# The inverse table's copy and clearing on VectorE, and the first weight loads dealt out anew

## The chip, the cores and the metric

One core of a Trainium2 chip runs the kernel. The metric is the device time of one execution in microseconds (us). The kernel before takes 508.08 us, the median of three runs (507.65, 508.08 and 508.6).

## The reference

The reference is a forward pass and its gradients. Sequence length is S = 2048, width D = 512, hidden width F = 1376, all in bf16.

```python
xn = layernorm(q)                                     # [2048, 512]
kv = v * sum_t k[s - t] * shift_k[:, t]               # 4 taps
y  = causal_conv(kv, ssm_k) + kv * ssm_D              # by FFT of length 4096, per channel
h  = sigmoid(xn @ w_gate) * (xn @ w_up)               # [2048, 1376]
out = q + (xn * y) * silu(h @ w_down)
# outputs: out, and with grad_out the gradients of
# q, k, v, shift_k, ssm_k, ssm_D, w_gate, w_up, w_down
```

## The kernel before

**Recording and ordering.** The kernel body does not emit instructions directly. Each call such as `nc.vector.tensor_copy` goes to a recorder (`Rec.add`), which notes what it reads and writes. At the end `Rec.order` simulates the five engines with a table of estimated durations, picks an order for every engine, chooses the PSUM banks and, for evacuations of PSUM (`evac`), the engine (ScalarE or VectorE). `Rec.emit` then writes the instructions in that order. So an edit to one engine or one DMA queue can change the order of instructions on all engines, as long as the planned times differ. In the profile nearly all instructions carry the line of the emitter, L568, and matmuls carry L566.

**Stages.** First come constants (sine and cosine tables for the FFT, made by `gen_fft_consts`), layer normalisation of q (`f_ln`), the gate and up projections (`f_gen`, in eight groups of 256 tokens) and the forward convolution (`strK` for the filter, `strV` for the signal, both with an FFT written as matmuls). All these streams are interleaved. Then `stepB` does the backward pass of the gated part, group by group: `z_gen` (down projection and silu gradient), `d_gen` (gradient of h), `x_gen` (gradient of xn). At last the weight gradients (`dW`) run beside the backward convolution (`frontC`, `backC`).

**The inverse table.** The backward convolution multiplies by `RT2`, a table of 128 partitions by 2 by 128 elements, built in `RT2_gen` during `stepB`, when the third group of `d_gen` has been recorded. A copy of a single element per partition (from `dzA`, into `RT2`) only serves as a dependency: it keeps the clearing from being placed before that part of `dzA` is written. Then the table is cleared, and four ScalarE copies of 32 partitions each fill in blocks of the first table `RT`. Before the change, the single-element copy and the clearing run on GpSimd. The table itself is used only much later, in `inv3w`.

**The first loads.** `ld_w(eng, f0, f1)` loads columns f0 to f1 of w_gate and w_up on the DMA queue of `eng`, as two DMAs. Before the change the columns 0 to 512 and 512 to 1024 are loaded on ScalarE's queue (four DMAs of 512 KB each), the rest (1024 to 1376, two DMAs of 352 KB) on SyncE's queue, behind the first 256 KB of q (`f_x(0)`) and the filter (`ld_KT(0)`, 512 KB). Two tiny loads, the column ssm_D (`Dcol_b`, 1 KB) and the shift weights (`skT`, 4 KB), run on GpSimd's queue, ssm_D first. The shift weights are used in `strV` by the VectorE multiply that builds `dg4` (128x512 elements); ssm_D is added to the filter by GpSimd in `strK`. GpSimd also computes the power −1/2 in `f_ln`, one instruction of 128x1 per 128 tokens, between VectorE's statistics and VectorE's normalisation. The transposed load of k (`ld_kT(0)`) is made to wait, through a single-element GpSimd copy, for the last part of w_up.

Of the kernel before, what the change touches and what calls it, by code (L numbers as in the profile page):

```python
# [17 lines left out]
P = 128  # L18
# [641 lines left out]
def kernel_impl(ctx, tc, A_q, A_k, A_v, A_shift_k, A_ssm_k, A_ssm_D, B_x, B_w_gate, B_w_up, B_w_down,  # L660
                grad_out, out_0, out_1, out_2, out_3, out_4, out_5, out_6, out_7, out_8, out_9):
    nc = tc.nc
# [34 lines left out]
    RT2 = Ring(ar, [2, 128]).ap  # L697
# [4 lines left out]
    skT = Ring(ar, [NG, 4]).ap  # L702
# [29 lines left out]
    def f_x(q):  # L732
        T[q]["xq"] = wd[:, 0:2, :] if q == 1 else xq_r.next()
        dma2(nc.sync, T[q]["xq"], qC[:, :, 2 * q:2 * q + 2, :])
# [172 lines left out]
    def ld_KT(cg):  # L907
        stA["KT", cg] = KT_r.next()
        nc.sync.dma_start(stA["KT", cg], A_ssm_k[cg * GW:(cg + 1) * GW, :])
# [19 lines left out]
    def ld_w(eng, f0, f1):  # L929
        for w, src in ((wg, B_w_gate), (wu, B_w_up)):  # L930
            eng.dma_start(w[:, :, f0:f1], src[:, f0:f1].rearrange("(db p) f -> p db f", p=P))
# [6 lines left out]
    nc.vector.memset(neghalf, -0.5)  # L938
    f_x(0)
    ld_w(nc.scalar, 0, 512)  # L940
    ld_w(nc.scalar, 512, 1024)
    nc.gpsimd.dma_start(Dcol_b, A_ssm_D.rearrange("(cg p) -> p cg", p=P))
    nc.gpsimd.dma_start(skT, A_shift_k.rearrange("(cg p) t -> p cg t", p=P))
    ld_KT(0)
    ld_w(nc.sync, 1024, F)
    f_x(1)
    nc.gpsimd.tensor_copy(kT[:, 16:17], wu[:, 3, F - 1:F])
# [186 lines left out]
    BQ = [6, 7, 3, 0, 4, 1, 5, 2]  # L1134
# [15 lines left out]
    dzA = dz_r.ap  # L1150
# [102 lines left out]
            nc.scalar.copy(skb[:, :, db * 128:(db + 1) * 128], pb[:].rearrange("p (d t) -> p t d", t=4))  # L1253

    def RT2_gen():
        nc.gpsimd.tensor_copy(RT2[:, 0, 0:1], dzA[:, 2 * BQ[1], 0:1])
        nc.gpsimd.memset(RT2, 0.0)
        for r in range(4):
            h = slice(32 * r, 32 * r + 32)
            nc.scalar.copy(RT2[h, :, 64 * (r % 2):64 * (r % 2) + 64], RT[h, 0:2, :])  # L1260

    def stepB():
        yield from z_gen(BQ[0])
        yield from z_gen(BQ[1])
        for n, q in enumerate(BQ):
            yield from d_gen(q)
            if n in (2, 3, 7):
                flags.add("d%d" % n)
                yield 1
            if n + 2 < 8:  # L1270
                b_ld(BQ[n + 2])
                b_ldg(BQ[n + 2])
            if n == 2:
                skb_gen()
                RT2_gen()
            if 1 <= n < 7:
                yield from z_gen(BQ[n + 1])
            if n == 6:
                flags.add("z15")
                yield 1  # L1280
            yield from x_gen(q)
            if n + 3 < 8:
                f_ld(BQ[n + 3])
            if n == 5:
                flags.add("x5")
                yield 1
# [244 lines left out]
@with_exitstack  # L1531
def kernel(
    ctx: ExitStack,
    tc: tile.TileContext,
    A_q: bass.AP,
    A_k: bass.AP,
    A_v: bass.AP,
    A_shift_k: bass.AP,
    A_ssm_k: bass.AP,
    A_ssm_D: bass.AP,  # L1540
    B_x: bass.AP,
    B_w_gate: bass.AP,
    B_w_up: bass.AP,
    B_w_down: bass.AP,
    grad_out: bass.AP,
    out_0: bass.AP,
    out_1: bass.AP,
    out_2: bass.AP,
    out_3: bass.AP,
    out_4: bass.AP,  # L1550
    out_5: bass.AP,
    out_6: bass.AP,
    out_7: bass.AP,
    out_8: bass.AP,
    out_9: bass.AP,
):
    kernel_impl(tc, A_q, A_k, A_v, A_shift_k, A_ssm_k, A_ssm_D, B_x, B_w_gate, B_w_up, B_w_down,
                grad_out, out_0, out_1, out_2, out_3, out_4, out_5, out_6, out_7, out_8, out_9)
# [30 lines left out]
```

## Time and profile before

| | |
|---|---|
| median of 3 runs | 508.08 us |
| lowest, highest | 507.65, 508.6 us |
| the profiled execution | 513.07 us, span 511.3 us, granted clock 0.983 |
| instructions | 13658 |
| TensorE busy | 462.3 us (90% of the span) |
| VectorE busy | 393.8 us (77%) |
| ScalarE busy | 274.9 us (54%) |
| GpSimd busy | 27.9 us (5%) |
| DMA moved | 112.74 MB, mean 221 GB/s |

In the profile PE is TensorE's matmuls, PEld its weight loads (which overlap the matmuls), DVE is VectorE, ACT ScalarE, POOL GpSimd and SP SyncE; ACTq, POOLq and SPq are the DMA queues of these engines, or their sequencers. The start of a line is its time in us from the span's start and its length; what stands in brackets at the end is the engine's idle time before it, and what ended that. A granted clock below 1 is TensorE running slower than it can. A profiled execution is some 5 us longer than the runs without a profile.

### The profile page before, as it was taken

How to read it: one execution, taken by the hardware profiler on the slowest of the kernel's cores; microseconds unless marked ns; L12 is line 12 of the kernel's file. 1: busy time of each engine (PE TensorE's matmuls, PEld its weight loads, DVE VectorE, ACT ScalarE, POOL GpSimd, SP SyncE). 2: the span in 40 equal slices, each digit the busy share in tenths (PEclk: the TensorE clock that was granted, in tenths of full speed). 3: DMA queues.
4: the chain of work that ended last, by engine and by line, in shares of the span. 5: the costliest groups of instructions: out<-in, count | busy, mean ns of one | idle time of the engine just before them, and what ended most of it. 6: DMA issues, size and time to landing. Idle time of an engine off the chain costs nothing.

```text
span 511.3 us, 13658 instructions
## 1 busy us (share of the span) xinstructions
PE 462.3 (90%) x5862; PEld 303.4 (59%) x5895; DVE 393.8 (77%) x658; ACT 274.9 (54%) x344; POOL 27.9 (5%) x50
## 2 busy tenths in 40 slices
PE   2999989999999967999999999999888869978997
PEld 2776857586758544565566556445454545656665
DVE  6788989758775695887998998649765789995770
ACT  5759787667665664144464257147544765164121
POOL 4101100000000031000000000100000000000000
PEclk9899999999999997999999999999998999999999
DMA  9999999946599988788969788995989898985666
GB/s 250 232 245 302 275 212 248 266 166 197 195 241 242 240 186 160 241 231 249 288 197 272 199 193 197 238 258 202 196 201 244 194 203 228 229 202 134 161 209 198
DMA packets 173813, 112.74 MB, mean 221 GB/s; under 512 B 101621, under 2 KB 157881, under 8 KB 173752
## 3 DMA queue, kind: packets, MB, share of 16 engines
q1 hardware_dynamic: 171288, 109.37, 86.0%
q10 hardware_dynamic: 2112, 2.10, 1.5%
q8 instruction: 46, 0.75, 0.6%
q0 software_dynamic: 352, 0.40, 0.3%
q14 instruction: 15, 0.12, 0.1%
HBM read 39.23 MB, written 47.62 MB: 170 GB/s over the span
## 4 chain that ended last, share of the span: by engine, by line
PE 72%; DVE 10%; issue 6%; DMA 5%; ACT 5%; POOL 2%; ACTq 0%; DVEq 0%; POOLq 0%
PE psum L566 72%; DVE slab L568 10%; ACT slab L568 5%; DMA slab<-slab 2%; DMA slab<-in_B_w_up_dram 2%; POOL slab L568 2%; DMA slab<-in_B_w_gate_dram 1%; PE psum L568 0%; ACTq L568 0%; DVEq L568 0%; POOLq L568 0%
## 5 line engine op out<-in xcount | busy, mean ns | idle before, releaser
L566 PE MATMUL psum<-slab 128*128 128x256 bf16 (+10 forms) x5853 | 460.9, 265 | 45.5 <-ACT slab L568 25.4
L566 PEld LDWEIGHTS <-slab 128*128 128x128 bf16 (+5 forms) x5886 | 302.7, 102 | 203.1 <-issue 67.7
L568 ACT CAST slab<-psum 128x1024 bf16<-128x1024 f32 (+6 forms) x263 | 216.6, 874 | 173.8 <-PE psum L566 157.7
L568 DVE TENSOR_TENSOR slab<-slab 128x1024 bf16<-128x1024 bf16 (+4 forms) x344 | 243.1, 759 | 36.6 <-ACT slab L568 18.3
L568 DVE CAST slab<-psum 128x1024 bf16<-128x1024 f32 (+1 forms) x31 | 36.7, 1187 | 31.7 <-PE psum L566 18.5
L568 ACT ACTIVATE slab<-psum 128x1024 bf16<-128x1024 f32 (+2 forms) x44 | 37.3, 854 | 32.2 <-PE psum L566 29.1
L568 DVE TENSOR_TENSOR slab<-psum,slab 128x1024 bf16<-128x1024 f32 (+2 forms) x28 | 28.2, 1006 | 13.4 <-PE psum L566 11.0
L568 DVE STREAM_TRANSPOSE slab<-slab 128x512 f32<-128x512 f32 x48 | 30.8, 684 | 3.6 <-ACT slab L568 3.5
L568 ACT ACTIVATE slab<-slab 128x512 bf16<-128x512 bf16 (+3 forms) x25 | 21.7, 888 | 16.4 <-DVE slab L568 16.3
L568 DVE SCALAR_TENSOR_TENSOR slab<-slab 128x512 bf16<-128x512 bf16 (+1 forms) x48 | 24.7, 530 | 3.9 <-ACT slab L568 3.4
L568 DVE TENSOR_SCALAR slab<-slab 128x1 f32<-128x1 f32 (+8 forms) x58 | 13.7, 270 | 1.4 <-POOL slab L568 0.9
L568 POOL TENSOR_TENSOR slab<-slab 128x1 f32<-128x1 f32 (+1 forms) x20 | 9.9, 509 | 77.8 <-DVE slab L568 66.2
L568 DVE BATCH_NORM_STATS2 slab<-slab 128x6 f32<-128x512 bf16 x16 | 10.3, 681 | 4.2 <-DMA slab<-in_A_q_dram 4.2
L568 POOL MEMSET slab<- 128x128 bf16 (+4 forms) x8 | 3.4, 429 | 174.5 <-PE psum L566 133.1
L568 POOL DMA_DIRECT2D slab<-slab x8 | 4.3, 535 | 153.3 <-DVE slab L568 153.3
L568 DVE SCALAR_TENSOR_TENSOR slab<-psum,slab 128x512 bf16<-128x512 f32 x10 | 6.7, 686 | 4.3 <-PE psum L566 4.3
L568 POOL COPY slab<-slab 128x1 bf16<-128x1 bf16 x2 | 6.9, 3426 | 48.4 <-DVE slab L568 42.9
L568 DVE COPY slab<-slab 128x1216 bf16<-128x1216 bf16 (+2 forms) x16 | 7.1, 460 | 1.1 <-ACT slab L568 1.1
L568 ACT ACT_TABLE_LOAD x2 | 2.6, 1283 | 5.7 <-DMA slab<-in_B_w_gate_dram 5.7
L568 ACT COPY slab<-slab 32x128 bf16<-32x128 bf16 x4 | 1.2, 295 | 5.4 <-POOL slab L568 5.3
L568 DVE MEMSET slab<- 32x192 uint32 (+2 forms) x7 | 1.1, 165 | 1.9 <-PEq L1573 0.8
L568 DVE BATCH_NORM_AGGREGATE slab<-slab 128x2 f32<-128x6 f32 x16 | 2.4, 170 | 0.0
(15 smaller groups left out, 11.5 us busy)
## 6 DMA issues: line engine op xcount, KB each, us to landing
KK_d<-slab SPq DMA_DIRECT2D x16, 512.0 KB, 4.0
slab<-KK_d SPq DMA_DIRECT2D x16, 512.0 KB, 5.2
out_dram<-slab SPq DMA_DIRECT2D x58, 128.0 KB, 3.2
hS_d<-slab SPq DMA_DIRECT2D x8, 704.0 KB, 5.8
dgS_d<-slab SPq DMA_DIRECT2D x8, 704.0 KB, 4.8
duS_d<-slab SPq DMA_DIRECT2D x8, 704.0 KB, 5.5
sF_d<-slab SPq DMA_DIRECT2D x6, 704.0 KB, 5.6
slab<-sF_d SPq DMA_DIRECT2D x6, 704.0 KB, 5.7
```

Of the source, the lines that this page charges most:

```text
L566: getattr(self.nc.tensor, m)(*[place(v) for v in aa], **{x: place(v) for x, v in kk.items()})
L568: getattr(getattr(self.nc, eng), meth)(*[place(v) for v in a], **{x: place(v) for x, v in k.items()})
```

## The change

In `RT2_gen` the single-element copy and the clearing move from GpSimd to VectorE. At the start, the weight columns 512 to 1024 are loaded on SyncE's queue, behind the filter and ahead of the columns from 1024 on, so that ScalarE's queue keeps two DMAs of 512 KB. On GpSimd's queue the shift weights are loaded ahead of ssm_D. Nothing else in the source changes. The order that the recorder finds does change: on TensorE from the 137th to about the 926th matmul, on the other engines in the same part and around the inverse table. Of the PSUM evacuations, two of 128x1024 elements are now given to ScalarE instead of VectorE. The four table copies of ScalarE now stand together, behind the casts that they stood among.

```diff
@@ kernel_impl, the first loads
     f_x(0)
     ld_w(nc.scalar, 0, 512)
-    ld_w(nc.scalar, 512, 1024)
+    nc.gpsimd.dma_start(skT, A_shift_k.rearrange("(cg p) t -> p cg t", p=P))
     nc.gpsimd.dma_start(Dcol_b, A_ssm_D.rearrange("(cg p) -> p cg", p=P))
-    nc.gpsimd.dma_start(skT, A_shift_k.rearrange("(cg p) t -> p cg t", p=P))
     ld_KT(0)
+    ld_w(nc.sync, 512, 1024)
     ld_w(nc.sync, 1024, F)
     f_x(1)
@@ RT2_gen
     def RT2_gen():
-        nc.gpsimd.tensor_copy(RT2[:, 0, 0:1], dzA[:, 2 * BQ[1], 0:1])
-        nc.gpsimd.memset(RT2, 0.0)
+        nc.vector.tensor_copy(RT2[:, 0, 0:1], dzA[:, 2 * BQ[1], 0:1])
+        nc.vector.memset(RT2, 0.0)
         for r in range(4):
             h = slice(32 * r, 32 * r + 32)
             nc.scalar.copy(RT2[h, :, 64 * (r % 2):64 * (r % 2) + 64], RT[h, 0:2, :])
```

## The prediction

> **What bounds the kernel now.** I read the page first (busy shares, the chain that ended last), then the chain in order of time, the waits around its one GpSimd piece, the timeline there, and last the first 30 us.
>
> ```profile
> span 511.3 us, 13658 instructions
> PE 462.3 (90%) x5862; PEld 303.4 (59%) x5895; DVE 393.8 (77%) x658; ACT 274.9 (54%) x344; POOL 27.9 (5%) x50
> PE 72%; DVE 10%; issue 6%; DMA 5%; ACT 5%; POOL 2%; ACTq 0%; DVEq 0%; POOLq 0%
> ```
>
> TensorE (PE) is busy for 90% of the span and makes 72% of the chain: the kernel is bound by TensorE, and what a change is worth is the TensorE idle time (and slow clock) that it removes. GpSimd (POOL) is busy for 5%, yet holds 2% of the chain. The chain in order of time shows one large POOL piece, and the timeline shows what happens around it:
>
> ```profile
> 186.74 6.67 POOL slab L568
> 195.32 5.41 PE psum L566 x33
> ...
> 183.30 5.41 PE L566 MATMUL psum<-slab 128*128 128x256 bf16 x52 [0.90 <-ACT slab L568]
> 183.77 9.59 DVE L568 TENSOR_TENSOR slab<-slab 128x512 bf16<-128x512 bf16 x20 [0.74 <-ACT slab L568]
> 186.74 6.67 POOL L568 COPY slab<-slab 128x1 bf16<-128x1 bf16 x1 [42.94 <-DVE slab L568]
> 186.99 1.50 ACT L568 CAST slab<-psum 128x1024 bf16<-128x1024 f32 x2 [0.38 <-PE psum L566]
> 193.47 0.31 POOL L568 MEMSET slab<- 128x256 bf16 x1
> 193.81 0.30 ACT L568 COPY slab<-slab 32x128 bf16<-32x128 bf16 x1 [5.32 <-POOL slab L568]
> 194.01 1.26 ACT L568 CAST slab<-psum 128x768 bf16<-128x768 f32 x2
> 194.83 1.63 DVE L568 TENSOR_TENSOR slab<-slab 128x768 bf16<-128x768 bf16 x3 [1.47 <-ACT slab L568]
> 195.32 8.87 PE L566 MATMUL psum<-slab 128*128 128x256 bf16 x48 [6.61 <-ACT slab L568]
> 199.85 4.24 DVE L568 TENSOR_TENSOR slab<-slab 128x1024 bf16<-128x1024 bf16 x7 [3.40 <-ACT slab L568]
> ```
>
> The reader sees a pile-up. GpSimd's copy of one element per partition (the first line of `RT2_gen`) starts at 186.74 and takes 6.67 us; it ends at 193.41, when VectorE's run of 20 multiplies (183.77 + 9.59 = 193.36) ends. ScalarE, in order, stands at its first inverse-table copy for 5.32 us waiting for GpSimd's memset, with two PSUM casts queued behind (194.01 to 195.27); TensorE needs the second of them and is idle for 6.61 us (188.71 to 195.32).
>
> **The change, part by part.** *(a) The table's copy and memset move to VectorE.* The same GpSimd copy elsewhere in the trace is short, and VectorE has rows for both kinds:
>
> ```profile
> L568 POOL COPY slab<-slab 128x1 bf16<-128x1 bf16 x1 | 0.2, 186 | 5.4 <-DMA slab<-in_B_w_up_dram 5.4
> L568 DVE COPY slab<-slab 128x1 bf16<-128x1 bf16 x4 | 0.6, 149 | 1.1 <-ACT slab L568 1.1
> L568 DVE MEMSET slab<- 32x192 uint32 x4 | 0.9, 218 | 1.1 <-PE psum L566 0.8
> L568 ACT COPY slab<-slab 32x128 bf16<-32x128 bf16 x4 | 1.2, 295 | 5.4 <-POOL slab L568 5.3
> ```
>
> So 186 ns grew to 6670 ns beside a full VectorE queue: 6.5 us of it is contention. VectorE gets one copy (0.15 us) and one memset (at most 0.22 us, from a shape with 1.5 times the elements per partition), 0.37 us together, on an engine that is idle in this stage (below).
>
> The Trainium skill, SBUF — State Buffer, section "Who interferes with whom", says that a VectorE instruction with two SBUF inputs contends with a GpSimd instruction that reads SBUF, and that the pair is held for the full instruction. Taken literally one multiply (9.59 us for 20, so 0.48 us on average) would be the whole wait and part (a) would be worth under 1 us; the trace's 6.67 us, ending with the run and not with an instruction, disagrees with that size, and the memset that only writes took its 0.31 us. The measurement decides.
>
> In the changed program's order the four ScalarE table copies no longer stand ahead of the two casts; they come some ten ScalarE instructions later. The order of TensorE from here to the end is as before. Without the copies the 128x768 cast can start when the cast before it ends (186.99 + 1.50 = 188.49; its matmuls are done by then, TensorE having stopped at 188.71) instead of at 194.01. Shift: 194.0 − 188.55 = 5.4 us. TensorE resumes at about 189.9, 1.2 us idle instead of 6.6.
>
> The idle time cost clock as well:
>
> ```profile
> 183.00:185.00 2.00, 1.70 (x16) 1.52 (x16) 1.22 (x5) 2.00 (x5) 0.00 (x0) 1.00 1.28 290
> 195.00:196.00 1.00, 0.68 (x4) 0.48 (x4) 1.00 (x3) 0.95 (x4) 0.00 (x0) 0.50 1.01 75
> 196.00:197.00 1.00, 1.00 (x7) 0.67 (x6) 0.46 (x1) 0.20 (x1) 0.00 (x0) 0.50 0.87 194
> 197.00:198.00 1.00, 1.00 (x6) 0.72 (x5) 0.00 (x0) 0.00 (x0) 0.00 (x0) 0.50 1.28 290
> 198.00:199.00 1.00, 1.00 (x9) 0.77 (x7) 0.00 (x0) 0.19 (x1) 0.00 (x0) 0.74 1.28 290
> ```
>
> (Columns: window, length, busy time of PE, PEld, DVE, ACT, POOL, then the granted clock, DMA share, GB/s.) From 195.32 to 199 TensorE works at 0.50 to 0.74: 0.68×0.5 + 2×0.5 + 0.26 = 1.6 us lost. The 0.90 us idle before 183.30 left the clock at 1.00, so I take no drop after 1.2 us. Together TensorE can be 5.4 + 1.6 = 7.0 us earlier.
>
> Is VectorE next late? It keeps its backlog to 193.36, so at once it can win only its own idle gaps, 1.47 + 3.40, less the added 0.37: 4.5 us. After that there is further slack, and TensorE does not stop:
>
> ```profile
> 200.00:240.00 40.00, 39.74 (x224) 21.49 (x228) 34.16 (x70) 14.91 (x20) 0.00 (x0) 1.00 0.81 233
> ```
>
> VectorE has 40 − 34.2 = 5.8 us of slack in 200 to 240, so it makes up the missing 2.5 us there; TensorE meanwhile runs on work that VectorE finished in its backlog. I take 0.5 us of the 7.0 as lost, so −6.5 us, with ends −4.5 and −7.0. At the copies' new place ScalarE already waits for VectorE and then for TensorE:
>
> ```profile
> 220.54 0.81 ACT L568 ACTIVATE slab<-slab 128x512 bf16<-128x512 bf16 x1 [0.76 <-DVE slab L568]
> 223.05 1.01 ACT L568 CAST slab<-psum 128x1024 bf16<-128x1024 f32 x1 [1.70 <-PE psum L566]
> ```
>
> Four copies of 0.295 us make 1.2 us against 0.76 + 1.70 us of idle time; what is queued behind is the activation at 220.54, later by at most 1.2 − 0.76 = 0.4 us, which VectorE awaits. Nothing if the 1.70 us covers it, 0.4 us if not; inside the 0.5 above. Later stages should keep the gain, since TensorE's order there is as before.
>
> *(b) The start.*
>
> ```profile
> 3.48 0.95 POOL L568 DMA_DIRECT2D slab<-in_A_ssm_D_dram  x1
> 5.70 1.28 ACT L568 ACT_TABLE_LOAD   x1 [5.70 <-DMA slab<-in_B_w_gate_dram]
> 10.88 0.71 DVE L568 TENSOR_TENSOR slab<-slab 128x512 bf16<-128x512 bf16 x1 [1.27 <-DMA slab<-in_A_shift_k_dram]
> 14.08 13.83 PE L566 MATMUL psum<-slab 128*128 128x256 bf16 x148 [0.71 <-DMA slab<-in_B_w_up_dram]
> 16.70 3.01 SPq L568 DMA_TRANSPOSE slab<-in_A_k_dram  x1
> 28.45 0.95 DVE L568 COPY slab<-slab 128x1216 bf16<-128x1216 bf16 x2
> slab<-in_A_ssm_D_dram POOLq DMA_DIRECT2D x1, 1.0 KB, 6.8
> slab<-in_A_shift_k_dram POOLq DMA_DIRECT2D x1, 4.0 KB, 6.4
> 12.00:14.00 2.00, 0.79 (x8) 0.51 (x9) 1.97 (x17) 2.00 (x4) 0.00 (x0) 1.00 1.14 332
> 14.00:16.00 2.00, 1.92 (x16) 1.73 (x16) 1.12 (x4) 0.59 (x2) 0.00 (x0) 0.55 1.11 270
> 14.00:40.00 26.00, 24.62 (x293) 19.68 (x293) 20.43 (x42) 17.05 (x20) 3.42 (x8) 0.93 1.06 246
> 40.00:65.00 25.00, 25.00 (x426) 18.84 (x425) 23.61 (x38) 19.57 (x22) 1.98 (x4) 1.00 0.97 267
> 65.00:90.00 25.00, 22.02 (x375) 16.96 (x374) 23.02 (x38) 20.38 (x23) 2.32 (x5) 1.00 1.09 243
> ```
>
> ScalarE could not begin its table load before 5.70 because its fourth weight load had to be issued first; with two loads it is free after its second issue. But the chain into the first projection (14.08) runs through VectorE: the normalisation stands behind the 128x512 multiply that waits for the shift weights (10.88), then the transposes and their cast on ScalarE. The tiny loads' exchange lets the shift weights land where the D column did, 3.48 + 6.8 = 10.3 instead of 10.8; but the changed order also puts that multiply one step ahead of the epsilon adds, so these now queue behind it. I net the two at zero, ±0.5 us.
>
> The loads that follow lose little: all bytes are the same, at worst 2 × 512 KB pass SyncE alone at the 270 GB/s seen with one queue (14 to 16) instead of the 332 seen with two (12 to 14): 1.05 MB × (1/270 − 1/332) = 0.7 us later for the last weights, and with them the transposed K load of 16.70, whose copy comes at 28.45. That is hidden: 28.45 − 16.70 leaves 11.7 us, its own landing included.
>
> The Trainium skill, DMA: Bandwidth & Descriptors, section "Issuing engines are not separate DMA queues", says loads from several engines share the same 16 DMA engines and only issue time is saved; by it the 0.7 us would be 0. The two rows differ in what they carry, so they cannot tell.
>
> Beyond that, the order on TensorE changes from its 137th to about its 926th matmul (some 430 are done by 40 us, 855 by 65 us, so until about 70 us), and two 128x1024 evacuations move from VectorE to ScalarE. That can win at most the idle time: 26 − 24.6 = 1.4 us, nothing in 40 to 65, and 3.0 us in 65 to 90, where VectorE is busy for 23.0 of 25 us. What a worse order could lose has no row; I bound it by about as much again as is idle now. I take 0, from −2 to +3.5.
>
> **Sum.** −6.5 + 0 = −6.5 us: span 511.3 → 504.8, the profiled execution 513.07 → 506.6. The plain runs' median is 508.08, 5 us under the profiled one; the pile-up is made by queue order, not by profiling, so I subtract the same: **501.6 us**.
>
> **Rivals.** *VectorE becomes the bound* (15%): it stays behind through 200 to 240 and the gain is only 4.5 us, 503.6. Against it: 5.8 us of slack in that stretch. *The new start order costs* (10%): the early idle of 1.4 + 3.0 us grows by 3.5 us, 505.1. *The contention goes elsewhere, or ScalarE meets the same stall at the new memset* (4%): 508.1, no change; against it, GpSimd has no other work near 187 us, and the new place has idle ScalarE. *Slower* (4%): the shift weights' load. VectorE's first normalisation now queues entirely behind the multiply that waits for it, and everything on TensorE behind the normalisation. Each us that it lands after 10.3 is a us on the end; it decides once it lands 6.5 us later, beyond 16.8, when a further 2 us gives 510. For it: it competes with megabytes of weights, all DMA engines busy. Against it: the same queue landed both tiny loads in 6.4 and 6.8 us under that pressure (DMA share over 1 in the rows above).
>
> **How the numbers follow.** The forecast has 67%. Its range is −9.0 (7.0 and a start that wins 2) to −4.5, 499.1 to 503.6; with the start rival the upper end is 505.1, which leaves out about 1 in 10 above and few below. 0.2% is 1.0 us, about what a measurement can tell from no change. All cases with a pure gain are faster: 0.93; same 0.03; slower 0.04.
>
> **What would show it.** Right: no GpSimd copy near 187; TensorE's gap there under 2 us, its clock 1.00 through the stretch; the chain without POOL there; the first long matmul run still starting within 0.5 us of 14.1. Wrong: a TensorE wait on ACT of over 3 us around 190, a VectorE wait chain in 195 to 240, or TensorE reaching the matmul group that now starts at 183.30 more than 2 us earlier or later (then it is the start that decides).

## The result, and the profile after

The changed kernel takes 502.54 us (median of four runs, 500.71 to 503.45), the kernel before 507.87 us beside it (four runs, 507.49 to 508.6). The ratio is 0.9889, with a 95% interval of 0.9857 to 0.9920: 5.6 us less of the 507.87 (4.1 to 7.3). The forecast was 501.6 us, in a range of 499.1 to 505.1. The profiled execution took 500.71 us, with a span of 498.9. The ratios here and below leave out the few executions in the chip's slower state (two of 17 of the kernel before and the 511.04 us of the last variant), while medians and ranges hold all.

The page of the changed kernel, its heads and the shares of the chain:

```profile
span 498.9 us, 13661 instructions
PE 461.0 (92%) x5862; PEld 303.7 (61%) x5895; DVE 391.1 (78%) x658; ACT 276.6 (55%) x346; POOL 21.0 (4%) x48
PE 71%; DVE 12%; issue 6%; ACT 6%; DMA 4%; POOL 1%; ACTq 0%; DVEq 0%; POOLq 0%
```

TensorE does the same work in a shorter span (92% instead of 90%). GpSimd is busy for 6.9 us less, which is the copy of 6.67 us and the memset of 0.31.

The timeline of the changed kernel around the place where the pile-up was (start, length, engine, line, operation, tile, count, idle time before and its releaser):

```profile
182.80 5.41 PE L566 MATMUL psum<-slab 128*128 128x256 bf16 x52 [0.90 <-ACT slab L568]
...
183.27 15.21 DVE L568 TENSOR_TENSOR slab<-slab 128x512 bf16<-128x512 bf16 x30 [0.74 <-ACT slab L568]
...
186.49 2.82 ACT L568 CAST slab<-psum 128x1024 bf16<-128x1024 f32 x4 [0.38 <-PE psum L566]
...
189.36 12.94 PE L566 MATMUL psum<-slab 128*128 128x256 bf16 x74 [1.15 <-ACT slab L568]
...
200.90 0.14 DVE L568 COPY slab<-slab 128x1 bf16<-128x1 bf16 x1
...
212.05 0.17 DVE L568 MEMSET slab<- 128x128 uint32 x1
...
212.25 1.22 ACT L568 COPY slab<-slab 32x128 bf16<-32x128 bf16 x4
...
215.55 1.01 ACT L568 CAST slab<-psum 128x1024 bf16<-128x1024 f32 x1 [1.24 <-PE psum L566]
```

ScalarE runs its four casts in one go, TensorE stands for 1.15 us instead of 6.61, and there is no GpSimd line. VectorE runs 30 multiplies in one go where it ran 20, then 3, then 7 with idle time between. The copy, the memset and ScalarE's four table copies come 14 to 19 us later, and ScalarE still has idle time behind them (1.24 us before the cast at 215.55).

The chain in order of time (start, length, piece) shows the same, and the window rows (window, length, busy time of PE, PEld, DVE, ACT, POOL, then granted clock, DMA share, GB/s) show a clock that doesn't drop:

```profile
182.80 5.20 PE psum L566 x48
188.00 0.02 issue
188.02 1.30 ACT slab L568 x2
189.32 0.04 issue
189.36 3.87 PE psum L566 x33
193.23 0.05 issue
193.28 10.54 PE psum L566 x54
```

and before

```profile
200.79 10.54 PE psum L566 x54
```

The windows of the changed kernel:

```profile
183.00:200.00 17.00, 15.80 (x117) 10.95 (x117) 16.70 (x34) 9.83 (x14) 0.00 (x0) 1.00 0.82 166
200.00:240.00 40.00, 39.74 (x243) 23.38 (x246) 34.71 (x76) 19.51 (x30) 0.00 (x0) 1.00 0.95 281
```

The same 33 matmuls take 3.87 us here and took 5.41 before: 1.54 us of clock. The piece behind them starts at 193.28 instead of 200.79, 7.51 us earlier. Of this 0.50 is there already at the group of 182.80 (183.30 before), and 7.0 is the pile-up. It is kept for at least 140 us: a group of 59 matmuls that both timelines show comes at

```profile
342.44 5.49 PE L566 MATMUL psum<-slab 128*128 128x512 bf16 x59 [0.16 <-issue]
```

before, and after at

```profile
334.93 5.49 PE L566 MATMUL psum<-slab 128*128 128x512 bf16 x59 [0.16 <-issue]
```

again 7.51 us earlier. The two spans differ by 12.4 us, so 4.9 us more separate the two profiles behind this point, where both kernels have the same order on TensorE. The waits of TensorE from 200 us on (waited for: total, times, longest), before and after:

```profile
PE psum L566 <- issue: 11.0, 11, 2.3
```

```profile
PE psum L566 <- issue: 5.9, 9, 2.5
```

Waits for which the profile shows no releaser are 5.1 us longer in the profile of before. It is scatter and no effect of the change, since both kernels have the same order there and the same sum is 6.3 us in a kernel that keeps the pile-up and 8.5 in a second profile of the changed kernel (both below).

### The profile page after: what moved, and what is told of

Read it like the earlier page. It is cut to its first block, busy times and chain, and to the rows that moved or that the text cites. A ratio compares the mean times of both kernels' runs of the same rounds, so it can differ in the third digit from the quotient of the medians.

```text
span 498.9 us, 13661 instructions
## 1 busy us (share of the span) xinstructions
PE 461.0 (92%) x5862; PEld 303.7 (61%) x5895; DVE 391.1 (78%) x658; ACT 276.6 (55%) x346; POOL 21.0 (4%) x48
## 4 chain that ended last, share of the span: by engine, by line
PE 71%; DVE 12%; issue 6%; ACT 6%; DMA 4%; POOL 1%; ACTq 0%; DVEq 0%; POOLq 0%
PE psum L566 71%; DVE slab L568 12%; ACT slab L568 6%; DMA slab<-slab 3%; DMA slab<-in_A_shift_k_dram 1%; POOL slab L568 1%; PE psum L568 0%; ACTq L568 0%; DVEq L568 0%; POOLq L568 0%; POOLq L1573 0%
## 5 line engine op out<-in xcount | busy, mean ns | idle before, releaser
L566 PE MATMUL psum<-slab 64*128 64x128 bf16 (+10 forms) x5853 | 459.6, 266 | 34.5 <-ACT slab L568 16.9
L568 ACT CAST slab<-psum 128x1024 bf16<-128x1024 f32 (+4 forms) x265 | 218.2, 875 | 170.5 <-PE psum L566 153.6
L568 DVE CAST slab<-psum 128x1024 bf16<-128x1024 f32 (+1 forms) x29 | 34.1, 1183 | 28.4 <-PE psum L566 14.8
L568 POOL MEMSET slab<- 128x128 bf16 (+3 forms) x7 | 3.1, 446 | 219.6 <-PE psum L566 176.2
L568 DVE MEMSET slab<- 32x192 uint32 (+3 forms) x8 | 1.3, 165 | 1.9 <-PEq L1573 0.8
L568 PE MATMUL psum<-slab 128*4 128x128 bf16 (+1 forms) x9 | 1.7, 331 | 0.0
L568 POOL DMA_DIRECT2D slab<-in_A_shift_k_dram x2 | 1.5, 762 | 3.2 <-DMA sF_d<-slab 3.2
```

The lines of the kernel that those rows point to most:

```text
L566: getattr(self.nc.tensor, m)(*[place(v) for v in aa], **{x: place(v) for x, v in kk.items()})
L568: getattr(getattr(self.nc, eng), meth)(*[place(v) for v in a], **{x: place(v) for x, v in k.items()})
```

## The experiments

Every time is compared with runs of the kernel before on the same chip: 509.06 us (median of 17) for the first four kernels, 508.59 (median of 11) for the next three.

**Only the inverse table's part.** The first loads stay as before.

```diff
@@ RT2_gen
-        nc.gpsimd.tensor_copy(RT2[:, 0, 0:1], dzA[:, 2 * BQ[1], 0:1])
-        nc.gpsimd.memset(RT2, 0.0)
+        nc.vector.tensor_copy(RT2[:, 0, 0:1], dzA[:, 2 * BQ[1], 0:1])
+        nc.vector.memset(RT2, 0.0)
```

> The kernel before, with only the inverse table's copy and clearing moved to VectorE; the first loads as before. Theory (queue order: ScalarE stood behind a blocked GpSimd copy): TensorE's idle time near 188.7 us falls from 6.6 to about 1.2 us, the clock stays 1.00 through 200, TensorE reaches the group that began at 200.79 about 7 us earlier, and the whole kernel is 4 to 7 us faster than before. Rival (the gain comes from the new first loads): within 1 us of before, whatever the gap does.

Measured: 502.82 us (501.28 to 504.59), ratio 0.9882 (0.9841 to 0.9922). Its timeline:

```profile
183.20 5.41 PE L566 MATMUL psum<-slab 128*128 128x256 bf16 x52 [0.90 <-ACT slab L568]
189.76 50.43 PE L566 MATMUL psum<-slab 128*128 128x256 bf16 x304 [1.15 <-ACT slab L568]
```

The group of 183.30 stays within 0.1 us, the wait falls to 1.15 us, and the 59 matmuls come at 335.32, 7.1 us earlier. This part alone has the whole gain.

**Only the first loads.** The table's copy and clearing stay on GpSimd.

```diff
@@ kernel_impl
     ld_w(nc.scalar, 0, 512)
-    ld_w(nc.scalar, 512, 1024)
-    nc.gpsimd.dma_start(Dcol_b, ...)
     nc.gpsimd.dma_start(skT, ...)
+    nc.gpsimd.dma_start(Dcol_b, ...)
     ld_KT(0)
+    ld_w(nc.sync, 512, 1024)
```

> The kernel before, with only the first loads dealt out anew; the inverse table stays on GpSimd. Theory: the 6.6 us gap and the 0.50 clock after it stay; TensorE reaches the group of 183.30 about 0.5 us earlier, and the kernel is 0 to 1 us faster. Rival (the gain comes from the loads): 4 to 6 us faster.

Measured: 510.15 us (508.52 to 514.16, 12 runs), ratio 1.0026 (0.9994 to 1.0058): no gain, and a loss of up to 3 us isn't excluded. The forecast of 0 to 1 us less holds only at its lower end. Its timeline keeps the pile-up whole, 0.36 us earlier:

```profile
182.94 5.41 PE L566 MATMUL psum<-slab 128*128 128x256 bf16 x52 [0.90 <-ACT slab L568]
...
186.38 6.67 POOL L568 COPY slab<-slab 128x1 bf16<-128x1 bf16 x1 [42.94 <-DVE slab L568]
...
194.97 45.22 PE L566 MATMUL psum<-slab 128*128 128x256 bf16 x249 [6.61 <-ACT slab L568]
```

GpSimd's copy takes 6.67 us again, to the hundredth. The clock's loss isn't as constant: the 33 matmuls behind the stall took 6.06 us here and 5.41 in the profile of before, against 3.87 at full clock, so the 59 matmuls come at 342.74, 0.3 us later than before. This profile's issue waits from 200 us on are the 6.3 us named above, and its span is 507.6: 3.7 us under that of before, with the same stall in it.

**GpSimd keeps its work; ScalarE's copies are queued later.** This takes the contention and the queue apart. GpSimd still copies and clears, but the four ScalarE table copies are made to depend on the last PSUM cast of the third `d_gen`, so they no longer stand ahead of the casts. The orders of TensorE, VectorE and GpSimd are those of before.

```diff
@@ d_gen
-            nc.scalar.copy(dh[:, 0:nb, :], ps[:, 0:nb, :])
+            dlast[0] = nc.scalar.copy(dh[:, 0:nb, :], ps[:, 0:nb, :]).n
@@ RT2_gen, around the four ScalarE copies
+        last = dlast[0]
+        n0 = len(rec.ops)
         for r in range(4):
...
+        for op in rec.ops[n0:]:
+            op.deps.add(last)
```

> The kernel before, with GpSimd's copy and clearing where they were, and only ScalarE's four table copies made to wait for the third d_gen group, so that they no longer stand ahead of the two PSUM casts. Theory (it is the queue position on ScalarE that costs, not GpSimd's slow copy): GpSimd's copy still takes 6 to 7 us, TensorE's gap is nevertheless about 1.2 us, and the kernel is as fast as with the table on VectorE, 4 to 7 us under before. Rival (the contention itself costs, VectorE or TensorE being slowed by it): within 1 us of before.

Measured: 502.04 us (500.6 to 503.22), ratio 0.9865 (0.9824 to 0.9906). Its timeline:

```profile
184.67 15.21 DVE L568 TENSOR_TENSOR slab<-slab 128x512 bf16<-128x512 bf16 x30 [0.74 <-ACT slab L568]
...
187.64 12.29 POOL L568 COPY slab<-slab 128x1 bf16<-128x1 bf16 x1 [43.39 <-DVE slab L568]
...
190.76 49.56 PE L566 MATMUL psum<-slab 128*128 128x256 bf16 x300 [1.15 <-ACT slab L568]
```

GpSimd's copy is not shorter but nearly twice as long: 12.29 us, from 187.64 to 199.93, again to the end of VectorE's run (184.67 + 15.21 = 199.88). A length of 6 to 7 us was wrong, since ScalarE, no longer held, feeds VectorE ten more multiplies. The time is as good as that of the changed kernel all the same. So the slow copy costs nothing by itself; what cost was that ScalarE, in order, stood behind it with the casts.

**The changed kernel again, beside these.**

> The changed kernel once more, against the kernel before on the same chip. Up to 365 us the trace repeats the first one within 0.2 us (TensorE resumes at 189.4 after 1.15 us). Theory (the difference of 12.4 us between the two profiled executions, against 5.3 between the medians, is scatter in TensorE's issue waits after 365 us, 11.0 us in the trace before and 5.9 after): the issue waits after 200 us come out anywhere between 5 and 11 us, and the span follows them one to one; times 500.5 to 503.5, 5 to 6 us under before. Rival (the change itself shortens the late stage): issue waits again near 5.9 us, and times near 501.

Measured: 502.2 us (500.27 to 505.55, six runs), ratio 0.9869 (0.9818 to 0.9920): the time repeats. The trace was expected to repeat within 0.2 us and doesn't. Its timeline, and two windows of 3.41 us:

```profile
183.68 7.08 PE L566 MATMUL psum<-slab 128*128 128x256 bf16 x52 [0.90 <-ACT slab L568]
191.91 48.26 PE L566 MATMUL psum<-slab 128*128 128x256 bf16 x291 [1.15 <-ACT slab L568]
```

```profile
180.43:183.84 3.41, 2.51 (x15) 1.01 (x14) 2.91 (x6) 2.26 (x5) 0.00 (x0) 1.00 1.32 196
183.84:187.26 3.42, 3.42 (x18) 2.37 (x17) 3.07 (x9) 2.33 (x6) 0.00 (x0) 0.50 1.27 284
```

TensorE reaches the group 0.9 us later than in the first profile, and its clock drops to 0.50 behind the 0.90 us wait that left it at 1.00 there: the 52 matmuls take 7.08 us instead of 5.41. The other eight profiles of the kernel and its variants show no drop behind this wait. The drop costs 1.7 us, half of the 3.41 us for which it lasts. So the 59 matmuls come at 337.49 here, only 4.95 us earlier than before: the 7.0 us of the pile-up, less 1.67 for the drop and 0.38 for the later start of the group. The issue waits from 200 us on sum to 8.5 us, between the 5 and 11 that were expected, but the span doesn't follow them one to one: with 2.6 us more of them than in the first profile, the part behind the 59 matmuls is 1.2 us longer.

**The single-element copy on ScalarE, the clearing on GpSimd.**

```diff
-        nc.gpsimd.tensor_copy(RT2[:, 0, 0:1], dzA[:, 2 * BQ[1], 0:1])
+        nc.scalar.copy(RT2[:, 0, 0:1], dzA[:, 2 * BQ[1], 0:1])
         nc.gpsimd.memset(RT2, 0.0)
```

> The kernel before, with the single-element copy on ScalarE instead of GpSimd; the clearing stays on GpSimd, the loads and the order of TensorE and VectorE as before. Theory (VectorE's multiplies, with two inputs in SBUF, block a GpSimd instruction that reads SBUF): the clearing, which only writes, starts near 187 us and takes 0.3 us beside the same VectorE run; TensorE's gap is about 1.2 us and the kernel 4 to 7 us faster than before. Rival (any GpSimd instruction is held up by a busy VectorE): the clearing takes 6 to 7 us and the gap and the time are as before.

Measured: 504.19 us (500.04 to 505.74), ratio 0.9894 (0.9850 to 0.9937). Its timeline:

```profile
187.51 0.30 POOL L568 MEMSET slab<- 128x256 bf16 x1 [43.16 <-ACT slab L568]
...
190.43 49.78 PE L566 MATMUL psum<-slab 128*128 128x256 bf16 x307 [1.17 <-ACT slab L568]
```

GpSimd's memset runs in the middle of VectorE's multiplies and takes 0.30 us. So not all of GpSimd's work is held up there: the copy, which reads SBUF, was, and the memset, which only writes, isn't.

**The single-element copy left out.** Then nothing ties the clearing and the table copies to the late place.

```diff
-        nc.gpsimd.tensor_copy(RT2[:, 0, 0:1], dzA[:, 2 * BQ[1], 0:1])
```

> The kernel before, without the single-element copy: clearing (GpSimd) and table copies (ScalarE) then fall into the first 20 us. Theory: no GpSimd work and no table copy near 187 us, TensorE's gap about 1.2 us, 4 to 7 us faster than before; at the start ScalarE's four table copies (1.2 us) cost 0 to 0.5 us. Rival (the copies at the start delay the first projections): the matmul group of 183.30 comes over 1 us later and the gain is under 5 us.

Measured: 503.02 us (500.05 to 505.06), ratio 0.9876 (0.9837 to 0.9915). TensorE waits 1.15 us at 188.82, as in the others, and ScalarE makes the copies in the first 20 us (three at 16.04, 0.91 us together). So no place for them that is clear of the casts is better than another by more than these intervals.

**The changed kernel with the tiny loads in their old order.** ssm_D ahead of the shift weights, all else as changed.

> The changed kernel with the two tiny loads in their old order (ssm_D first); weight loads and inverse table as changed. It tells the two halves of the start apart. Theory (the two halves of the tiny loads' exchange cancel): VectorE's dg4 multiply waits for the shift weights until 10.8 us, behind the epsilon adds as before; the first long matmul group starts between 13.9 and 14.5 us, and the time is within 1 us of the changed kernel's. Rival (the exchange carries the start): the first projection is over 0.5 us late and the kernel 1 us or more slower than the changed one.

Measured: 504.63 us (502.2 to 511.04, four runs), ratio 0.9887 (0.9831 to 0.9944). The order on TensorE is another one for some 1750 matmuls here. VectorE's `dg4` multiply came at 10.87 us, as expected, and the first long run at 14.22, a little earlier than in the changed kernel. But TensorE comes to the late group some 3 us later:

```profile
185.78 5.41 PE L566 MATMUL psum<-slab 128*128 128x256 bf16 x52 [0.90 <-ACT slab L568]
```

The runs don't tell it from the changed kernel: both intervals hold both.

**What holds GpSimd.** Two kernels of their own measure GpSimd's 128x1 copy beside runs of VectorE instructions, and the first also bursts of matmuls with idle time between them.

```diff
+        def two(i):
+            nc.vector.tensor_tensor(o[:, i], a, b, ALU.mult)
...
+            nc.vector.tensor_copy(t[:, k + 1:k + 2], g[:, k:k + 1])
...
+                nc.gpsimd.tensor_copy(g[:, k + 1:k + 2], t[:, k + 1:k + 2])
...
+            for i in range(n):
+                f(i)
```

VectorE's copy of one element releases GpSimd's copy, and `f` is the run on VectorE, for multiplies the function `two`; lines between are left out.

> Not the kernel: a measurement that computes nothing of the reference. A GpSimd copy of 128x1 is released just ahead of runs of VectorE instructions of 128x512 bf16: none, 1, 4 and 16 multiplies with two SBUF inputs, 16 in a chain, 16 copies, 16 copies from PSUM, 16 multiplies of PSUM by SBUF; then a GpSimd clearing of 128x256 alone and beside 16 multiplies. Last, bursts of 60 matmuls with ScalarE chains of 0, 2, 4, 6 and 9 copies between them, twice. Theory (GpSimd waits for the end of the whole run, where the run uses its port): 0.2, 0.6, 1.6, 6 and 6 to 7 us for the first five, over 2 us beside the SBUF copies, 0.2 us beside both PSUM kinds; the clearing 0.3 us both times. Rival (held for one instruction at a time): under 1 us for all copies. Rival (any busy VectorE): 10 us beside the PSUM kinds and 6 us for the clearing. The clock: bursts after idle times under 3 us run at 1.00, those after 5 us and more start at 0.50.

Measured in the first: 0.19 us with no run, 0.31 beside 1 multiply and beside 4, 5.34 beside 16, 0.31 beside a chain of 16 in which each multiply reads the result of the one before, and 0.19 beside 16 copies from SBUF, 16 copies from PSUM and 16 multiplies with one input in PSUM. A memset took 0.31 us alone and beside 16 multiplies. Three that were expected long were short: 4 multiplies (1.6 us expected), the chain (6 to 7) and the copies from SBUF (over 2). The timeline, for the copy beside 16 multiplies, beside those with an input in PSUM, and for a copy behind the second memset:

```profile
4.58 5.45 DVE L63 TENSOR_TENSOR o<-a,b 128x512 bf16<-128x512 bf16 x16
4.73 5.34 POOL L82 COPY g<-t 128x1 bf16<-128x1 bf16 x1 [1.09 <-DVE t L80]
...
30.54 0.19 POOL L82 COPY g<-t 128x1 bf16<-128x1 bf16 x1 [9.44 <-DVE t L80]
...
42.09 0.28 POOL L94 COPY g<-big 128x1 bf16<-128x1 bf16 x1
```

The long time of the kernel is back without the kernel: the copy ends with the run (10.07 and 10.03). But the last line is a copy that reads SBUF 0.5 us into another unbroken run of 16 multiplies (it began at 41.58), and it took 0.28 us. So the memset's 0.31 us beside that run says nothing: there a reading copy wasn't held either. The bursts have 60 matmuls, of which 59 take 12.90 us at full clock. After 0.74 us of idle time they took 12.90 both times; after 2.04 us 14.58 and 12.90; after 3.34 us 14.58 both times. After 4.64 us already the first matmul is slow (0.61 us instead of 0.39) and the rest took 15.01 and 15.14. A full clock after any wait under 3 us, as expected, didn't hold. Windows of 3.41 us around the two waits of 2.04 us (columns as above) show what differs:

```profile
77.00:80.41 3.41, 1.37 (x7) 0.60 (x7) 0.00 (x0) 1.80 (x4) 0.00 (x0) 1.00 0.00 0
80.41:83.83 3.42, 3.42 (x10) 1.21 (x9) 0.00 (x0) 0.00 (x0) 0.00 (x0) 0.50 0.00 0
...
165.74:169.16 3.42, 1.49 (x7) 0.49 (x5) 0.00 (x0) 1.75 (x4) 0.00 (x0) 1.00 0.00 0
169.16:172.57 3.41, 3.30 (x16) 1.54 (x17) 0.00 (x0) 0.05 (x1) 0.00 (x0) 1.00 0.00 0
```

The clock went to 0.50 at 80.41 and back at 83.83. The other drops between these bursts begin whole multiples of 3.41 us later, and each lasts one or two such steps. Cut in the same steps, the first wait leaves TensorE busy for 1.37 of 3.41 us, 40%, and the next step is slow. The second wait runs over the end of a step: that step is busy for 1.49 us, 44%, and no drop follows. In this pair it isn't the length of the wait that decides, but how much of it falls into one step. The drop in the second profile of the changed kernel can be read alike: of the 2.51 us that TensorE was busy from 180.43 to 183.84, 1.03 are four matmuls with a single row of weights, and without them the step is busy for 43%. That such matmuls count for little is a guess that no run tests.

The second kernel repeats the doubtful forms at five sizes (512 down to 384 elements), and releases GpSimd ahead of the run or behind four of its instructions.

```diff
+            nc.vector.tensor_copy(t[:, 40 + k:41 + k], g[:, k:k + 1])
+            for i in range(lead):                                     # lead is 0 or 4
+                f(i, n)
+            nc.vector.tensor_copy(t[:, k + 1:k + 2], t[:, 40 + k:41 + k])
+            nc.gpsimd.tensor_copy(g[:, k + 1:k + 2], t[:, k + 1:k + 2])
+            for i in range(lead, 16):
+                f(i, n)
```

> Not the kernel, and computing nothing of the reference: the first measurement's GpSimd copy again, five times each with VectorE instructions of 512, 480, 448, 416 and 384 elements, to see how often a copy is held. First a release just ahead of 16 multiplies with two SBUF inputs, then a release behind four of them, then the same in a chain (each waits for the one before), then the same with SBUF-to-SBUF copies. Theory (a chance at every gap between VectorE instructions, which a run without waits may or may not give): the copies beside multiplies split into short ones (0.2 to 0.7 us) and long ones that end with the run (3 to 6 us); all five in a chain are short; all five beside copies short. Rival (held to the end of the run whenever it starts inside one): all ten beside multiplies without waits are long. Rival (one instruction at a time): all twenty under 1 us, and the 5.34 us before was another cause.

Measured, from 512 elements to 384: released ahead of the 16 multiplies 0.31 down to 0.25 us; behind four of them 4.00, 3.80, 3.60, 3.40, 3.20; in a chain 0.38 down to 0.31; behind four of 16 copies from SBUF 2.40, 2.30, 2.20, 2.10, 2.00. The first of each kind in the timeline, two of them with VectorE's run:

```profile
2.51 0.31 POOL L77 COPY g<-t 128x1 bf16<-128x1 bf16 x1 [2.07 <-DVE t L76]
...
29.00 4.11 DVE L63 TENSOR_TENSOR o<-a,b 128x512 bf16<-128x512 bf16 x12
29.15 4.00 POOL L77 COPY g<-t 128x1 bf16<-128x1 bf16 x1 [5.52 <-DVE t L76]
...
55.05 5.49 DVE L66 TENSOR_TENSOR o<-o,b 128x512 bf16<-128x512 bf16 x12
55.14 0.38 POOL L77 COPY g<-t 128x1 bf16<-128x1 bf16 x1 [2.03 <-DVE t L76]
...
88.01 2.40 POOL L77 COPY g<-t 128x1 bf16<-128x1 bf16 x1 [5.28 <-DVE t L76]
```

It is the form that decides, not chance: five of five are alike in each group. A GpSimd copy released behind four instructions of a run that VectorE goes through without a pause waits to the end of the run. Where each VectorE instruction waits for the one before (the chain: 5.49 us for 12 multiplies instead of 4.11), the copy gets in after about one of them. What was expected of the copies from SBUF, short as in the first kernel, was wrong.

What stays open is the copy released just ahead of a run: long beside the first kernel's 16 multiplies, short beside the second's. The traces show a difference that may explain it. Ahead of the first kernel's long copy VectorE had gone through four multiplies and the releasing copy without a pause (3.18 to 4.60 us, 4.51, then the run at 4.58). In the second kernel the releasing copy had to wait for the copy before it, 0.18 us behind it (7.73 and 7.91). All short copies beside multiplies with two SBUF inputs or beside copies from SBUF, the one at 42.09 too, came at most three VectorE instructions behind such a pause, and all long ones at least five. No run varies that alone, so it is a pattern and not shown as the cause.

## Why the prediction was right

**The pile-up, the main term.** It said: TensorE's wait from 6.61 to about 1.2 us, no clock drop, 7.0 us earlier. Measured: 1.15 us, clock 1.00, 7.0 us. The rival that the contention or the stall goes elsewhere falls with the first experiments: the table part alone gives 0.9882, the load part alone 1.0026. One link of the account becomes sharper. The prediction counted "6.5 us of it is contention", and the kernel with the later ScalarE copies shows 12.3 us of contention at no cost. The price came from the order on ScalarE together with the contention: without the order it cost nothing, and without the contention (the copy on ScalarE, TensorE's wait 1.17 us) the order cost nothing.

**VectorE next late, 0.5 us.** It wasn't: the 7.51 us of 193.28 are still 7.51 at the 59 matmuls. In the second profile of the changed kernel, too, the 4.96 us of 195.83 are 4.95 there. The rival of a gain of only 4.5 us is excluded for this stretch by these profiles, not by the times, whose interval (4.1 to 7.3 us) holds it; 200 to 240 us show TensorE busy for 39.74 of 40 us, as before. The term was mis-sized by 0.5 us.

**The costs on VectorE and ScalarE.** 0.14 and 0.17 us against 0.15 and at most 0.22; the four ScalarE copies took 1.22 us against 1.2 and lie in idle time.

**The start, 0.** The first long run of matmuls came at 14.39 instead of 14.08, inside the 0.5 us, and the late group 0.50 us earlier. Two further profiles of this order have it 0.36 us earlier and 0.38 later, so 0 with 0.5 either way is what the runs show, and the first profile's 0.50 us is luck. By the times, the load part alone lies between 0.3 us less and 3.0 us more (0.9994 to 1.0058 of 509.06), so the rival's 3.5 us is just outside. One term looks wrong in this pair of profiles: the last weights, which release a GpSimd copy, landed

```profile
17.83 0.19 POOL L568 COPY slab<-slab 128x1 bf16<-128x1 bf16 x1 [5.70 <-DMA slab<-in_B_w_up_dram]
```

1.34 us later (16.49 before) and not at most 0.7. It stays hidden, as said. But one pair of profiles doesn't size it: in the four further kernels with the old order of the weights the same copy came between 15.55 and 18.42 us (16.58, 17.23, 18.42, 15.55), in the three with the new order at 17.70, 17.62 and 17.42. The means, 16.85 of five and 17.64 of four, are 0.8 us apart, with 2.9 us of scatter among the first. So the 0.7 us of the prediction, and the 0 that follows from the rule of the Trainium skill weighed there (DMA: Bandwidth & Descriptors, "Issuing engines are not separate DMA queues"), can't be told apart by these runs.

**The clock assumption.** That 1.2 us of idle time bring no drop held in all seven profiles with a wait of 1.15 or 1.17 us there: the clock is 1.00 behind each. But it was taken from the 0.90 us wait that left the clock at 1.00, and behind that very wait the clock dropped in one profile of nine. So the conclusion held, while one trace couldn't carry it: a wait so short cost nothing or 1.7 us, and by the windows above it is where it falls in the 3.41 us steps that seems to tell which. The term of 1.6 us for the drop behind the pile-up measured 1.54 us in the profile of before and 2.19 in that of the loads alone.

The Trainium skill (TensorE: Matmul & The Clock Gate, "What's actually happening") has the clock halved after an idle window of about 3.4 us that runs freely. The steps of 3.41 us in these traces agree with its length; that a step in which TensorE was busy for 40% is enough doesn't agree with an idle window, and the measurement decides.

**From the profiled execution to the median.** The profiled execution of before stood 5 us over the median and that difference was taken as a constant. It isn't one, and neither is it a rule that a profiled execution is some 5 us longer: the changed kernel's profiled execution is its fastest run. What was long is the late stage of that one execution: behind the 59 matmuls it takes 168.9 us, and 164.0 to 166.0 in the other five profiles that show this group. The issue waits go the same way and may be most of it (11.0 us there, 5.9 here, 6.3 to 8.8 in the other seven profiles). Subtracting a local difference of 6.5 from the median was still right, since these waits belong to neither kernel; comparing the two spans would have given 12.4 us, twice the effect. The 6.5 us lie inside both intervals: 4.1 to 7.3 us in the first comparison, and in the second 4.1 to 9.3 (0.9818 to 0.9920 of 509.06).

**The contention.** The Trainium skill (SBUF — State Buffer, "Who interferes with whom") says which pairs interfere, and the runs agree on each pair that they settle. Multiplies with two SBUF inputs (4.00 us) and copies from SBUF (2.40 us) hold GpSimd's copy, inputs from PSUM don't (0.19 us), and GpSimd's memset isn't held in the midst of multiplies (0.30 us, with the copy on ScalarE). The Trainium skill says there, too, that the pair is held for the full instruction. There the measurement decides: 6.67, 12.29, 5.34 and 4.00 us are the lengths of what was left of whole runs.

No version beats the changed kernel clearly. All six that keep ScalarE's casts free lie between 0.9865 and 0.9894, each inside the others' intervals.

## What to carry to other kernels

A tiny instruction on an idle engine is not free when an in-order engine waits for it ahead of urgent work: look at what is queued behind the waiter. Here any of four cures gave the same 5 to 7 us: another engine, another place in the queue, a write in place of a read, or no dependency at all. When two profiles are compared, compare the time at a landmark shortly behind the change, and the issue waits of the rest, before the spans.

## What was not expected of the hardware

- GpSimd's 0.19 us copy lasted to the end of an unbroken run of VectorE instructions, up to 12.29 us, not for one instruction. Plain copies from SBUF hold it too (2.40 us); a chain with pauses doesn't (0.38 us), and neither did a run that had begun just before, behind a pause (0.25 to 0.31 us).
- TensorE's clock dropped to 0.50 behind a wait of 0.90 us in one profile of nine. In the measuring kernel a wait of 2.04 us brought a drop when it left one step of 3.41 us busy for 40%, and none when it left it busy for 44%; a drop of one step costs 1.7 us.
- TensorE's waits that the profile gives to no releaser, after 200 us, ranged from 5.9 to 11.0 us over kernels that run the same matmuls there. Some of 0.16 us stand where matmul records are missing; those of 1 to 2.5 us remain in traces with all 5895 matmuls. What they are isn't shown.
